# A Strassen scheme of seven products for the first matrix product of the second gated MLP

## The chip, the cores and the metric

The kernel runs on one core of a Trainium2 chip. The metric is device time in microseconds (us) of one execution, the median of three runs. A core has five engines with a queue of instructions each: TensorE (PE) for matrix products, VectorE (DVE), ScalarE (ACT) and GpSimd (POOL) for elementwise work, and SyncE (SP), which here only issues DMA transfers. PE reads SBUF and writes PSUM; ACT and DVE read both.

## What is computed

The input passes an attention with exponential gates (mLSTM, 4 batches x 8 heads x 768 steps, head size 40), whose output is a matrix of 3072 tokens x 320. Then come two MLPs, each of two matrix products with a function between them:

```
def _moe_ref(x, w_in, w_out):            # first part
    h = x @ w_in                         # 3072x320 @ 320x2048
    g = np.where(h >= 1, h, np.where(h <= -1, 0.0, (h + 1) ** 2 / 4))
    return g @ w_out                     # 3072x2048 @ 2048x320

def _moe2_ref(x, w_in, w_out):           # second part
    h = x @ w_in
    r = np.maximum(h, 0.0)
    g = r * r
    return g @ w_out
```

Both parts have the same shapes. Everything is float32 on the outside.

## The kernel before

Tokens are cut into 24 chunks of 128, d_ff into 16 tiles of 128 (f). The model size 320 is three pieces: 128, 128 and 64 rows. PE takes a shortened float format, so every float32 operand is split into a high part and a low part (high = cast, low = value minus high), and a product is three matmuls: high x high, high x low, low x high. The 64 rows left over stand twice in one stationary operand, once as high and once as low, so they need two matmuls. A first product of one tile f with one block of tokens (`mm1` in `dense`, L1131) is thus 3 + 3 + 2 = 8 matmuls; the weight tile is the stationary operand, and the columns of a matmul are the tokens of the block. The second product (`mm2`, L1191) takes 128 tokens as stationary operand and 320 columns of w_out: three matmuls for each chunk and tile, added up in PSUM over the tiles.

In the first part, blocks have 3 chunks (384 columns), in the second part 4 (512 columns, 6 blocks, `SIZES2`). One `dense(j, f)` is a visit of block j to tile f: mm1 into a PSUM bank h (there are two), then relu on ACT (L1136, L1138), in the first part a square (L1142), a product with h on DVE (`gate`, L1149, L1151), the cast to the high part on ACT (a copy, L485), the subtraction for the low part (`lo`, L1163, on POOL or DVE), and mm2. In the second part all subtractions of `lo` run on POOL. The accumulators of mm2 are the PSUM banks acc0, acc1, acc2 and v.

Weight tiles of both parts take the same 16 places w0 to w15. They come as 64-bit numbers (`weights`): a DMA load into wraw, a clamp (L508), a move (`a_move`, L503) and a tail pass (`a_tail`, L511) on ACT, a join on DVE (L515), the cast (`a_hi`, to w), and two subtractions (L524, L528) for the low parts. A tile of the second part can be written once the last block of the first part has used its place. So two blocks at the seam are visited in turns of eight tiles (`TURNS2`), two of the first part and, before the change, also the first two of the second part.

The order on each engine is not that of the code. Every step is given to `Plan.add` with engine or engines, rank, duration, needs and products; `Plan.order` then goes through a list schedule: an engine that is free takes, of the steps that are ready, the one with the lowest rank. Ranks are moved by tables (`MOVE`, `SHIFT_OF`, `FINE`), the choice between engines by `PICK` and by `PEN`, a surcharge on any engine but the first named. Engines then work through their queues in that order, waiting on semaphores. Attention (chunk by chunk) runs in between the visits of the first part and is over well before the second part.

Of the kernel before, what the change touches and what calls it, by code (L numbers as in the profile page):

```python
# [19 lines left out]
U = 64  # L20
# [19 lines left out]
class Plan:  # L40
# [18 lines left out]
    def add(self, eng, rank, dur, fn, need=(), make=()):  # L59
# [10 lines left out]
        if self.group:  # L70
            bias = PICK.get(f"{kind}{i}", {}).get(fn.__name__, 0.0)
        self.bias.append(bias)
        self.tags.append(self.group)
        self.steps.append((eng, round(rank, 3), fn, tuple(need), tuple(make)))

# [3 lines left out]
    def order(self):  # L79
# [103 lines left out]
def pool(n):  # L183
# [13 lines left out]
LEAD2 = {3: [12, 9, 3], 4: [12, 9, 6, 3]}  # L197
# [14 lines left out]
}  # L212
# [16 lines left out]
        "keep": -54.24, "evac": -38.36, "turn": -51.89, "store": 169.37},  # L229
}  # L230
# [129 lines left out]
    "w15": {"clamp": -92.87, "a_hi": 47.78},  # L360
}
# [7 lines left out]
WLEAD2 = (13, 0)  # L369
# [15 lines left out]
def kernel(  # L385
# [15 lines left out]
        vt=2, qt=2, kt=2, sg=2, xn=2, rc=2, cx=2, yx=1, Ca=CA, Cb=CB, tiny=1, xTh=XTB, xTl=XTB, pa=PAB, r=3, g0=3, g1=3, o=2, x2=2,  # L401
        h=2, acc0=1, acc1=1, acc2=1, s=2, v=1)
    psum = ("h", "acc0", "acc1", "acc2", "s", "v")
    pools = {}
    for space, tags in ((None, [t for t in bufs if t not in psum]), (PS, psum)):
        for b in sorted({bufs[t] for t in tags}):
            kw = {} if space is None else {"space": space}
            pool_ = ctx.enter_context(tc.tile_pool(name=f"p{b}{'s' if space else ''}", bufs=b, **kw))
            for t in tags:
                if bufs[t] == b:  # L410
                    pools[t] = pool_
    const = ctx.enter_context(tc.tile_pool(name="const", bufs=1))
# [6 lines left out]
    eyes = const.tile([128, 8, U], F32, name="eyes")  # L419
    nident = const.tile([128, 128], F32R, name="nident")  # L420
    half = const.tile([128, 1], F32, name="half")
    it = const.tile([128, NCB, R], F32, name="it")
    logs = const.tile([128, SUMC + 1, 2, R], F32, name="logs")
# [28 lines left out]
    rest = [(j, 0, NF) for j in range(len(blocks)) if j not in turns]  # L452
    m = max(j for j, _, _ in TURNS1)
    n = max(j for j, _, _ in TURNS2)
    visits = TURNS1 + [x for x in rest if m < x[0] < n] + TURNS2 + [x for x in rest if x[0] > n]
    rank_of, first_of, ends, last_of, first_use = {}, {}, {}, {}, {}
    g = 0
    for j, f0, f1 in visits:
        first_of.setdefault(j, g)
        for f in range(f0, f1):  # L460
            rank_of[j, f], ends[j, f] = g, (f0, f1)
            last_of[blocks[j][0], f] = g
            first_use.setdefault((blocks[j][0], f), g)
            g += 1

# [27 lines left out]
    def weights(part, f, rank):  # L493
# [42 lines left out]
        plan.add(av(WH), rank, 0, a_hi, [("wt", K, 3)], [(W, part + 1)])  # L536
# [518 lines left out]
    def part2(j):  # L1055
        return blocks[j][0] == 1

    def xkeys(j, k):
        if part2(j):
            return [("qk", ("x", j), k), ("d0", ("x", j), k)], [("vko", ("x", j), k), ("d1", ("x", j), k)]  # L1060
        return [("xTh", j, k)], [("xTl", j, k)]

    def to_xT(j, k, src, at, key=None):
# [10 lines left out]
        def halves(i, s):  # L1074
            return [(t[:, :, s] if t.shape[1] > 1 else t[:, 0, s], slice(o, o + t.shape[1]) if t.shape[1] > 1 else o)
                    for t, o in xT[j][i]]

        def hi(e, i=0):
            if k == 0:
                tags = [("xTh", "xTl")] if blocks[j][0] == 0 else [("qk", "vko"), ("d0", "d1")]  # L1080
                xT.setdefault(j, {})[i] = [
                    (new(t[i], [128, n, w], F32R), o)
                    for t, (n, w, o) in zip(tags, [(3, NX, 0)] if len(tags) == 1 else [(2, NMAX, 0), (1, NMAX, 2)])]
            if i == 0:
                for t, c in halves(0, slice(L * k, L * (k + 1))):
# [23 lines left out]

    def dense(j, f):  # L1110
        part, mine = blocks[j]
# [5 lines left out]
        W = [(f"w{f}", part + 1, i) for i in (1, 2)]  # L1117

        def mm1():
            w = t_["w", part, f]["w"]  # L1120
            xh, xl = ([t[:, i, 0:N] for t, o in x for i in range(t.shape[1])] for x in xT[j].values())
# [11 lines left out]
        def relu():  # L1133
            r = z["r"] = new("r", [128, NX])[:, 0:N] if part == 0 else new("xTl", [128, NMAX])[:, 0:N]
            if part == 0:
                nc.scalar.activation(out=r, in_=z["h"], func=ACTF.Relu, scale=0.5, bias=half)  # L1136
            else:
                nc.scalar.activation(out=r, in_=z["h"], func=ACTF.Relu)  # L1138
# [7 lines left out]
        def gate():  # L1146
            r = z["r"]
# [252 lines left out]
```

## Time and profile before

| | us |
|---|---|
| median of 3 runs (827.82 to 828.53) | 828.47 |
| span of the profiled execution | 830.9 |
| PE busy | 819.8 |
| ACT busy | 459.0 |
| DVE busy | 387.1 |
| POOL busy | 365.8 |
| DMA, mean rate | 88 GB/s |

The profiled execution's own time is its span, 2.4 us above the median of the timed runs. Matmuls overlap in the profile, and their ends are modelled, so the pace of PE is read from the distance between starts, not from a duration. The second part begins with the first matmul of 512 columns, near 475 us, and the last matmul of the kernel starts near 827 us.

### The profile page before, as it was taken

How to read it: one execution, taken by the hardware profiler on the slowest of the kernel's cores; microseconds unless marked ns; L12 is line 12 of the kernel's file. 1: busy time of each engine (PE TensorE's matmuls, PEld its weight loads, DVE VectorE, ACT ScalarE, POOL GpSimd, SP SyncE). 2: the span in 40 equal slices, each digit the busy share in tenths (PEclk: the TensorE clock that was granted, in tenths of full speed). 3: DMA queues.
4: the chain of work that ended last, by engine and by line, in shares of the span. 5: the costliest groups of instructions: out<-in, count | busy, mean ns of one | idle time of the engine just before them, and what ended most of it. 6: DMA issues, size and time to landing. Idle time of an engine off the chain costs nothing.

```text
span 830.9 us, 18844 instructions
## 1 busy us (share of the span) xinstructions
PE 819.8 (99%) x7536; PEld 753.4 (91%) x7536; DVE 387.1 (47%) x760; ACT 459.0 (55%) x897; POOL 365.8 (44%) x387
## 2 busy tenths in 40 slices
PE   8999999999899999999999999999999999999998
PEld 7668899999899999999999988999899898998997
DVE  5678879785676555544225655312121111111111
ACT  4667678866456556555678867443433433433432
POOL 3133220042353467682677566534533534433333
PEclk9899999999999999999999999999999999999999
DMA  8467564435443464521313541002110100100000
GB/s 229 162 220 237 166 172 151 141 108 124 109 116 92 110 150 125 160 56 31 70 41 99 164 98 67 1 0 70 29 42 1 45 26 1 52 1 0 32 1 33
DMA packets 93244, 73.41 MB, mean 88 GB/s; under 512 B 58944, under 2 KB 77372, under 8 KB 93156
## 3 DMA queue, kind: packets, MB, share of 16 engines
q1 hardware_dynamic: 93156, 72.21, 30.5%
q8 instruction: 59, 0.97, 0.5%
q14 instruction: 29, 0.24, 0.1%
HBM read 61.67 MB, written 10.51 MB: 87 GB/s over the span
## 4 chain that ended last, share of the span: by engine, by line
PE 91%; DMA 4%; SPq 1%; DVE 1%; ACT 1%; POOL 1%; issue 0%; POOLq 0%; DVEq 0%
PE h L1131 42%; PE acc L1191 34%; PE v L1191 5%; PE v L904 2%; PE s L850 2%; PE acc L1274 1%; PE s L857 1%; PE h L745 1%; DMA qk<-in_qk_dram 1%; DMA w<-in_gates_dram 1%; DMA vko<-in_vko_dram 1%; PE acc L550 1%; PE h L748 1%; SPq L433 1%; DMA x<-xn 1%
## 5 line engine op out<-in xcount | busy, mean ns | idle before, releaser
L1163 POOL TENSOR_TENSOR xTh<-xTl,xTh 128x512 fp32r<-128x512 f32 x96 | 124.1, 1292 | 177.1 <-ACT xTh L485 176.8
L1191 PE MATMUL acc<-w,g 128*128 128x320 f32 x1152 | 194.9, 312 | 0.1
L1151 DVE TENSOR_TENSOR xTl<-xTl,h 128x512 f32<-128x512 f32 x96 | 66.0, 688 | 245.3 <-ACT xTl L1138 245.3
L1191 PEld LDWEIGHTS acc<-w,g 128*128 128x128 f32 x1152 | 176.0, 188 | 3.3 <-ACT g L485 0.6
L1131 PE MATMUL h<-xTh,w 128*128 128x384 f32 x640 | 176.1, 340 | 2.4 <-ACT xTh L485 2.3
L1191 PE MATMUL acc<-w,xTh 128*128 128x320 f32 x864 | 142.5, 308 | 0.0
L1191 PEld LDWEIGHTS acc<-w,xTh 128*128 128x128 f32 x864 | 134.2, 188 | 8.2
L1131 PE MATMUL h<-qk,w 128*128 128x512 f32 x384 | 135.9, 395 | 0.0
L1131 PE MATMUL h<-xTl,w 128*128 128x384 f32 x384 | 129.9, 338 | 0.6 <-POOL xTl L1092 0.6
L1138 ACT ACTIVATE xTl<-h 128x512 f32<-128x512 f32 x96 | 57.4, 598 | 115.2 <-PE h L1131 112.1
L1131 PEld LDWEIGHTS h<-xTh,w 128*128 128x128 f32 x640 | 117.3, 188 | 3.8 <-ACT xTh L485 2.6
L1136 ACT ACTIVATE r<-h,half 128x384 f32<-128x384 f32 x128 | 74.0, 578 | 79.6 <-PE h L1131 68.2
L1149 DVE SCALAR_TENSOR_TENSOR r<-r,h 128x384 f32<-128x384 f32 x128 | 70.0, 547 | 78.8 <-ACT r L1142 73.5
L485 ACT ACTIVATE xTh<-xTl 128x512 fp32r<-128x512 f32 x96 | 60.7, 632 | 81.9 <-PE v L1191 80.1
L1131 PEld LDWEIGHTS h<-qk,w 128*128 128x128 f32 x384 | 72.1, 188 | 12.9
L1163 POOL TENSOR_TENSOR g<-r,g 128x384 fp32r<-128x384 f32 x63 | 66.3, 1053 | 36.0 <-ACT g L485 35.2
L485 ACT ACTIVATE g<-r 128x384 fp32r<-128x384 f32 x128 | 66.4, 520 | 21.2 <-PE acc L1191 18.3
L1131 PE MATMUL h<-vko,w 128*128 128x512 f32 x192 | 75.7, 394 | 0.0
L1131 PEld LDWEIGHTS h<-xTl,w 128*128 128x128 f32 x384 | 72.4, 188 | 0.9 <-POOL xTl L1092 0.9
L1142 ACT ACTIVATE r<-r 128x384 f32<-128x384 f32 x128 | 66.9, 523 | 2.9
L1131 PE MATMUL h<-d,w 128*128 128x512 f32 x192 | 60.3, 395 | 0.0
L1191 PE MATMUL v<-w,xTh 128*128 128x320 f32 x288 | 57.8, 309 | 0.0
(148 smaller groups left out, 1098.4 us busy)
## 6 DMA issues: line engine op xcount, KB each, us to landing
wraw<-in_wts_dram SPq DMA_DIRECT2D x32, 704.0 KB
vko<-in_vko_dram SPq DMA_DIRECT2D x24, 524.5 KB
d<-f_all SPq DMA_DIRECT2D x32, 128.0 KB
qk<-in_qk_dram SPq DMA_DIRECT2D x24, 160.0 KB
out_dram<-o SPq DMA_DIRECT2D x20, 160.0 KB
qk<-in_qk_dram SPq DMA_DIRECT2D x24, 128.0 KB
x<-x SPq DMA_DIRECT2D x24, 128.0 KB
ab<-a_all SPq DMA_DIRECT2D x20, 128.0 KB
```

Source lines behind the costliest of these rows:

```text
L433: nc.sync.dma_start(out=to[a], in_=t[32 * a:32 * a + 32].rearrange("r (b t) -> r b t", t=32))
L485: nc.scalar.activation(out=out, in_=in_, func=ACTF.Copy)
L850: nc.tensor.matmul(out=z["s"][a][u, U * h:U * h + U], lhsT=z["qk"][row[a], 0, h, u], rhs=z["qk"][row[a], 1, h, u], start=True, stop=True)
L904: nc.tensor.matmul(out=z["y"][sub[u], E * h:E * h + E], lhsT=lhsT, rhs=rhs, start=start, stop=True, skip_group_check=True)
L1131: nc.tensor.matmul(out=h, lhsT=a, rhs=b, start=(i == 0), stop=(i == 7))
L1136: nc.scalar.activation(out=r, in_=z["h"], func=ACTF.Relu, scale=0.5, bias=half)
L1138: nc.scalar.activation(out=r, in_=z["h"], func=ACTF.Relu)
L1142: nc.scalar.activation(out=z["r"], in_=z["r"], func=ACTF.Square)
L1149: nc.vector.scalar_tensor_tensor(out=r, in0=r, scalar=1.0, in1=z["h"], op0=ALU.min, op1=ALU.max)
L1151: nc.vector.tensor_mul(out=r, in0=r, in1=z["h"])
L1163: engine[e].tensor_sub(out=z["g1"], in0=z["r"], in1=z["g0"].bitcast(F32))
L1191: nc.tensor.matmul(out=acc[k][:, 0:DM], lhsT=a, rhs=b, start=(f == f0 and i == 0), stop=(f == f1 - 1 and i == 2))
```

## The change

The second part's first product is no longer computed tile by tile. Two weight tiles (u = 0, 1; a pair p) and two token halves (a, b) of a block of six chunks form a 2 x 2 by 2 x 2 product, where the inner index is the first and the second piece of 128 rows of the model size. A scheme of seven products (Strassen's, in Winograd's form) replaces the eight. It needs four sums of the tokens (`operands`, tile tt or o, then split into th, tl), and sums of the weights (`sums_of`: one piece is summed in place in the odd tile, three sums go to ws). The 64 rows left over are added the plain way, two matmuls for each of the four results, inside the products P2, P5, P4 and P3. So a pair and block has 7 x 3 + 4 x 2 = 29 matmuls of 384 columns (`products`, L1424), where before the same work was 32 of 384 or 24 of 512.

The four results come together in the two banks of h (X and Y). P1 goes to X and ACT copies it (`first`, to a tile U); P2 is added to X and gives C11, which ACT reads through a relu. P6 goes to Y, DVE adds the copy (u2), P7 is added to Y, DVE adds the copy again (u3). P5 overwrites X, DVE adds u3 (C22); P4 is added to Y, DVE adds the copy (C21); P3 is added to X, DVE adds u2 (C12). Each result is then squared after a relu (`square`, L1473 and L1474 on ACT), cast (`hi`, L532) and subtracted (`lo`, L1484) into a tile G, and goes through mm2 (L1501) one pair later. Six accumulators are used: acc0, acc1, acc2, v and both banks s.

Blocks of the second part are four of six chunks, all run from pair 0 to pair 7, so the turns of the second part's blocks are gone. Pools are given back and taken anew in SBUF when attention is done (`swap1`) and when the first part's first products are done (`swap2`). The operands of every second block are put into the tiles g, r, wraw and wt, which the first part no longer uses. The surcharge `PEN` does not hold for the new steps (`EVEN`), so their subtractions may go to DVE, and in the built program all of `lo` does. The ranks of the new steps have tables of their own ("u", "z", "p").

```diff
-SIZES2 = [4] * 6
+SIZES2 = [6] * 4
+HB = 3
-TURNS2 = [(6, 0, 8), (7, 0, 8), (6, 8, 16), (7, 8, 16), (8, 0, 8), (9, 0, 8), (8, 8, 16), (9, 8, 16)]
+TURNS2 = [(6, 0, 8), (7, 0, 8), (6, 8, 16), (7, 8, 16)]
+PAIR = 4.0
+STAGE = {"P1": 0.0, "P6": 0.35, 0: 0.7, "P2": 1.05, "P7": 1.4, 1: 1.75, "P5": 2.1, "P4": 2.5, 2: 2.9, "P3": 3.3, 3: 3.65}
...
-                end = max(free.setdefault(e, 0.0) + ahead, ready[i]) + dur + (PEN if best else self.bias[i])
+                end = max(free.setdefault(e, 0.0) + ahead, ready[i]) + dur + ((0.0 if self.tags[i] and self.tags[i][0] in EVEN else PEN) if best else self.bias[i])
...
+        def apart(e):
+            u, v, s = y["t"], z["t"], sums()
+            engine[e].tensor_sub(out=s[:, 256:384], in0=u[:, 0:128], in1=v[:, 0:128])
+            engine[e].tensor_sub(out=s[:, 384:512], in0=u[:, WS:WH], in1=v[:, WS:WH])
+        def chain(e):
+            u, v, s = y["t"], z["t"], sums()
+            engine[e].tensor_add(out=v[:, 0:128], in0=v[:, 0:128], in1=v[:, 128:256])
+            engine[e].tensor_sub(out=s[:, 0:128], in0=v[:, 0:128], in1=u[:, 0:128])
+            engine[e].tensor_sub(out=s[:, 128:256], in0=u[:, 128:256], in1=s[:, 0:128])
...
+        def sums(e):
+            t = z["t"] = new(tt, [128, 4, L])
+            a, b = z[0], z[1]
+            for o, x, y in ((0, b[:, 0], a[:, 0]), (2, b[:, 1], b[:, 0]), (1, b[:, 1], t[:, 0]), (3, a[:, 1], t[:, 1])):
+                engine[e].tensor_sub(out=t[:, o], in0=x, in1=y)
...
+                seq = [(ah, bh), (ah, bl), (al, bh)]
+                if extra:
+                    seq += [(rest(extra[0]), x) for x in right(*extra[1])]
...
+        stage("P1", "X", 2, (0, 0), ("a", 0), None, [], [X])
+        plan.add({A: act(NH), V: dvep(NH)}, g + 0.1, 0, first, [X] + sw, [p1])
+        stage("P6", "Y", 2, (2, 0), ("t", 1), None, [], [Y_])
+        plus("u2", g + 0.4, "Y", "p1", "U", "u2", [Y_, p1])
+        stage("P2", "X", 0, (0, 1), ("a", 1), (0, ("a", 2)), [X, p1], [X + (1,)])
+        plan.add(A, g + 1.1, act(NH), relu, [X + (1,)] + sw, [("R", (q, "C11"))])
+        stage("P7", "Y", 0, (2, 2), ("t", 2), None, [Y_, u2], [Y_ + (1,)])
+        plus("u3", g + 1.5, "Y", "p1", "U", "u3", [Y_ + (1,), p1])
+        stage("P5", "X", 1, (1, 0), ("t", 0), (1, ("b", 1)), [X + (1,), ("R", (q, "C11"))], [X + (2,)])
+        plus("c22", g + 2.2, "X", "u3", "R", "C22", [X + (2,), u3])
+        stage("P4", "Y", 0, (1, 1), ("t", 3), (1, ("a", 2)), [Y_ + (1,), u3], [Y_ + (2,)])
+        plus("c21", g + 2.6, "Y", "p1", "R", "C21", [Y_ + (2,), p1])
+        stage("P3", "X", 0, (2, 1), ("b", 0), (2, ("b", 1)), [X + (2,), ("R", (q, "C22"))], [X + (3,)])
+        plus("c12", g + 3.4, "X", "u2", "R", "C12", [X + (3,), u2])
...
+            plan.add({A: act(NH) * (1 if C == "C11" else 2), **pv(NH)}, g + at, 0, square, [RK], [RK + (1,)])
+            plan.add(av(NH), g + at + 0.1, 0, hi, [RK + (1,)] + sw, [GK])
+            plan.add(pv(NH), g + at + 0.2, 0, lo, [RK + (1,), GK], [GK + (1,)])
```

On PE, in the last block before the change, one tile's first product and the second product of the tile before it stand in a row like this (qk, vko and the two d hold the tokens, xTh the second product's left side):

```order
L1131 MATMUL h<-qk,w_7639 128x512
L1131 MATMUL h<-vko,w_7639 128x512
L1131 MATMUL h<-qk,w_7639 128x512 x2
L1131 MATMUL h<-vko,w_7639 128x512
L1131 MATMUL h<-qk,w_7639 128x512
L1131 MATMUL h<-d_9268,w_7639 128x512
L1131 MATMUL h<-d_9276,w_7639 128x512
L1191 MATMUL acc_9877<-w_7433,xTh 128x320 x3
L1191 MATMUL acc_9883<-w_7433,xTh 128x320 x3
L1191 MATMUL acc_9903<-w_7433,xTh 128x320 x3
L1191 MATMUL v<-w_7433,xTh 128x320 x3
```

And on PE in the last block after it, the first half of a pair: P1, P6, P2, P7, P5 with the beginning of P4, where g, r, wraw and wt hold the block's tokens and sums, ws the weight sums, and G the second product's left side of the pair before:

```order
L1424 MATMUL h<-g,w_7634 128x384 x3
L1501 MATMUL acc_10116<-w_7533,G 128x320 x3
L1424 MATMUL h<-wraw,ws_7778 128x384 x3
L1424 MATMUL h<-g,w_7634 128x384 x3
L1424 MATMUL h<-r,w_7634 128x384 x2
L1501 MATMUL acc_10129<-w_7533,G 128x320 x3
L1424 MATMUL h<-wraw,ws_7778 128x384 x3
L1501 MATMUL acc_10154<-w_7533,G 128x320 x3
L1424 MATMUL h<-wraw,w_7802 128x384 x3
L1424 MATMUL h<-g,w_7802 128x384
L1424 MATMUL h<-wt,w_7802 128x384 x4
L1424 MATMUL h<-r,w_7802 128x384 x2
```

The products now alternate between the two banks h, and only one group of the second product and P6 stand between P1 and P2, where before a bank was read only after a whole tile's product.

On ACT, the place where the second part begins, before (xTl takes the relu, xTh the cast, wt, wraw and w are steps of weight tiles):

```order
L1138 ACTIVATE xTl<-h 128x512
L485 ACTIVATE g_7310<-r 128x384
L485 ACTIVATE xTh<-xTl 128x512
L1138 ACTIVATE xTl<-h 128x512
L511 ACTIVATE wraw<-wraw 128x704
L1138 ACTIVATE xTl<-h 128x512
L485 ACTIVATE xTh<-xTl 128x512
L485 ACTIVATE w_7368<-wt 128x704
```

The same place on ACT after (U is the copy of P1, R the relu, g and r without h are the first part's last visits, g and r from x are tokens of the next block):

```order
L532 ACTIVATE U<-h 128x384
L1244 ACTIVATE r<-r 128x384
L550 ACTIVATE wt<-wraw 128x704
L532 ACTIVATE w_7209<-wt 128x704
L1447 ACTIVATE R<-h 128x384
L532 ACTIVATE g<-r 128x384
L1474 ACTIVATE R<-R 128x384
L550 ACTIVATE wt<-wraw 128x704
L532 ACTIVATE G<-R 128x384
L532 ACTIVATE w_7253<-wt 128x704
L532 ACTIVATE g<-x_6646 128x2x128
L532 ACTIVATE r<-x_6646 128x128
```

The weight steps have kept their place at the seam, and between them now stand the copy, the relu, and up to eleven passes for each pair.

On DVE, a place in the first part where the order begins to differ, near the fourth visit, before:

```order
L1149 SCALAR_TENSOR_TENSOR r<-r,h 128x384
L891 TENSOR_TENSOR d_1110<-s,d_1110 128x256
L881 TENSOR_TENSOR Cb<-s,cx 104x164
L876 TENSOR_TENSOR cx<-Cb,ab 104x164
L1163 TENSOR_TENSOR g_1434<-r,g_1324 128x384
L811 TENSOR_TENSOR kt<-vko,d_1394 128x320
L774 SCALAR_TENSOR_TENSOR d_1453<-d_1116,eyes 128x512
```

and after, where kt comes later and a weight tile's clamp stands in between:

```order
L1249 SCALAR_TENSOR_TENSOR r<-r,h 128x384
L969 TENSOR_TENSOR Cb<-s,cx 104x164
L964 TENSOR_TENSOR cx<-Cb,ab 104x164
L555 TENSOR_SCALAR wraw<-wraw 128x704
L862 SCALAR_TENSOR_TENSOR d_1453<-d_1128,eyes 128x512
```

So the planner's other steps and tiles have moved steps of the first part against each other, though the tables of ranks of that part are unchanged.

## Rows read from the trace of the kernel before

**Rows 1.** The page: busy time by engine, and two rows of the 40 slices.

```profile
PE 819.8 (99%) x7536; PEld 753.4 (91%) x7536; DVE 387.1 (47%) x760; ACT 459.0 (55%) x897; POOL 365.8 (44%) x387
...
PEclk9899999999999999999999999999999999999999
```

**Rows 2.** Stretches: us, busy us of PE, PEld, DVE, ACT, POOL, PEclk, DMA share, GB/s.

```profile
80.00:100.00 20.00, 19.96 (x294) 16.84 (x291) 16.68 (x39) 13.38 (x29) 7.08 (x7) 1.00 0.47 145
...
120.00:140.00 20.00, 19.89 (x123) 19.11 (x123) 18.85 (x38) 16.11 (x39) 0.68 (x1) 1.00 0.32 104
...
420.00:440.00 20.00, 20.00 (x127) 20.00 (x126) 5.27 (x10) 16.34 (x41) 15.60 (x20) 1.00 0.17 48
...
540.00:560.00 20.00, 20.00 (x114) 18.15 (x113) 4.13 (x6) 9.17 (x19) 7.42 (x7) 1.00 0.00 0
...
700.00:720.00 20.00, 20.00 (x112) 18.02 (x111) 4.13 (x6) 9.53 (x22) 11.00 (x13) 1.00 0.10 31
```

**Rows 3.** PE in order of time, second part: start us, us, instruction, count.

```profile
599.73 0.39 PE L1131 MATMUL h<-qk,w 128*128 128x512 f32 x1
...
601.59 1.48 PE L1191 MATMUL acc<-w,xTh 128*128 128x320 f32 x9
...
818.62 1.48 PE L1191 MATMUL acc<-w,xTh 128*128 128x320 f32 x9
...
826.97 0.60 PE L1191 MATMUL v<-w,xTh 128*128 128x320 f32 x3
```

**Rows 4.** PE in order of time, first part, where attention is over.

```profile
406.95 0.34 PE L1131 MATMUL h<-xTh,w 128*128 128x384 f32 x1
...
447.63 0.33 PE L1131 MATMUL h<-xTh,w 128*128 128x384 f32 x1
```

**Rows 5.** Groups by line: busy us, mean ns of one, idle before and its releasers.

```profile
L1131 PEld LDWEIGHTS h<-xTh,w 128*128 128x128 f32 x640 | 117.3, 188 | 3.8 <-ACT xTh L485 2.6 <-DVE r L1149 0.5
L1136 ACT ACTIVATE r<-h,half 128x384 f32<-128x384 f32 x128 | 74.0, 578 | 79.6 <-PE h L1131 68.2 <-POOL g L1163 4.7 <-DVE g L1163 4.1
L1149 DVE SCALAR_TENSOR_TENSOR r<-r,h 128x384 f32<-128x384 f32 x128 | 70.0, 547 | 78.8 <-ACT r L1142 73.5 <-POOL d L1092 2.2 <-ACT g L485 1.7
L485 ACT ACTIVATE g<-r 128x384 fp32r<-128x384 f32 x128 | 66.4, 520 | 21.2 <-PE acc L1191 18.3 <-DVE o L1222 1.2 <-DVE r L1149 0.6
...
L1163 DVE TENSOR_TENSOR g<-r,g 128x384 fp32r<-128x384 f32 x65 | 41.7, 641 | 7.1 <-ACT g L485 6.7
...
L515 DVE SCALAR_TENSOR_TENSOR wt<-wt,wraw 128x704 int32<-128x704 int32 x32 | 31.8, 999 | 9.9 <-ACT wt L503 9.5
L511 ACT ACTIVATE wraw<-wraw 128x704 int32<-128x704 uint8 x32 | 27.2, 850 | 8.1 <-DMA wraw<-in_wts_dram 8.1
L503 ACT ACTIVATE wt<-wraw 128x704 f32<-128x704 f32 x32 | 26.5, 840 | 1.3 <-DVE w L528 1.1
L485 ACT ACTIVATE w<-wt 128x704 fp32r<-128x704 f32 x25 | 19.6, 785 | 3.7 <-DVE wt L515 3.4 <-PE acc L1191 0.2
```

**Rows 6.** All engines in order of time, near the end (idle before, releaser).

```profile
814.75 0.40 PE L1131 MATMUL h<-d,w 128*128 128x512 f32 x1
...
815.25 0.60 ACT L1138 ACTIVATE xTl<-h 128x512 f32<-128x512 f32 x1 [1.29 <-PE h L1131]
...
826.75 1.82 SPq L1235 DMA_DIRECT2D out_dram<-pa  x4
...
827.61 0.44 ACT L485 ACTIVATE pa<-v 128x320 f32<-128x320 f32 x1
```

**Rows 7.** The longest wait of PE, in order of time.

```profile
227.77 0.52 ACT L485 ACTIVATE xTh<-x 128x384 fp32r<-128x384 f32 x1 [4.70 <-DMA x<-xn]
...
228.34 0.45 PE L1131 MATMUL h<-xTh,w 128*128 128x384 f32 x1 [2.30 <-ACT xTh L485]
```

**Rows 8.** Two stretches of 2 us around it, columns as in rows 2.

```profile
226.00:228.00 2.00, 0.04 (x1) 0.00 (x0) 0.00 (x0) 0.23 (x1) 0.00 (x0) 1.00 0.51 161
...
230.00:232.00 2.00, 2.00 (x18) 1.56 (x20) 0.81 (x3) 0.22 (x1) 2.00 (x3) 0.50 0.07 23
```

More of the change, by code (lines that the diff above doesn't have):

```diff
@@ L74, in add, with marked @@
         self.steps.append((eng, round(rank, 3), fn, tuple(need), tuple(make)))
+    def marked(self, kind):
+        keys = []
+        for i, tag in enumerate(self.tags):
+            if tag and tag[0] == kind:
+                keys.append(("done", i))
+                self.steps[i] = self.steps[i][:4] + (self.steps[i][4] + (keys[-1],),)
+        return keys
     def mode_of(self, i):
@@ L229 @@
         "keep": -54.24, "evac": -38.36, "turn": -51.89, "store": 169.37},
+    "u": {"load": -10.31, "clamp": 38.18, "a_move": 169.88, "a_tail": 757.89, "v_join": -59.97, "a_hi": 720.77,
+        "v_lo": -372.19, "lo": 57.21, "apart": -172.84, "chain": -299.51, "s_hi": -216.6, "s_last": -370.46,
+        "s_lo": 1196.1},
[4 rows of a table added]
 }
@@ L360 @@
     "w15": {"clamp": -92.87, "a_hi": 47.78},
+    "u": {"clamp": -68.75, "a_hi": -219.76, "lo": 44.72, "apart": 161.63, "chain": -96.62, "s_hi": 111.69,
+        "s_lo": -17.71},
+    "z": {"sums": -189.49, "hi": -0.37, "lo": -1.49},
+    "p": {"first": -280.65, "square": -13.55, "hi": -127.32, "lo": 1.09, "evac": -259.63},
 }
@@ L451 @@
     turns = {j for j, _, _ in TURNS1 + TURNS2}
[L452 to L456, printed above, removed]
+    visits = TURNS1 + [(j, 0, NF) for j in range(NB1) if j not in turns] + TURNS2
+    rank_of, first_of, ends, last_of = {}, {}, {}, {}
     g = 0
@@ L461 @@
             rank_of[j, f], ends[j, f] = g, (f0, f1)
-            last_of[blocks[j][0], f] = g
-            first_use.setdefault((blocks[j][0], f), g)
+            last_of[f] = g
             g += 1
+    NP = NF // 2
+    pair_at = {}
+    for j in range(NB1, len(blocks)):
+        for p in range(NP):
+            pair_at[j, p] = g + PAIR * len(pair_at)
+    end_at = g + PAIR * len(pair_at)
     plan = Plan(bufs)
@@ L1133, in relu @@
         def relu():
[L1134 to L1138, printed above, removed]
+            z["r"] = new("r", [128, NX])[:, 0:N]
+            nc.scalar.activation(out=z["r"], in_=z["h"], func=ACTF.Relu, scale=0.5, bias=half)
         def square(e):
@@ L1213, in dense @@
-                continue
-            y = t_["o", part, n] = {}
-            end = j == len(blocks) - 1
-            def evac(e, k=k, y=y, n=n, end=end):
-                y["o"] = new("pa" if end else "o", [128, DM])
-                if f0:
-                    nc.vector.tensor_add(out=y["o"], in0=acc[k][:, 0:DM], in1=t_["pa", part, n])
-                elif part == 0:
-                    nc.vector.transpose(out=y["o"], in_=acc[k][:, 0:DM])
-                else:
-                    copy(e, y["o"], acc[k][:, 0:DM])
@@ L1226, in turn @@
-            def turn(y=y, n=n):
-                p = t_["pa", part, n]
-                nc.vector.transpose(out=p, in_=y["o"])
-                y["o"] = p
-            def store(n=n, y=y):
-                if part == 0:
-                    scatter(x2_d[n], y["o"])
-                else:
-                    nc.sync.dma_start(out=out[128 * n:128 * (n + 1), :], in_=y["o"])
-            ok = ("pa" if end else "o", (part, n))
-            on = {V: dvep(DM)}
-            if part and not f0 and not (end and k == 1):
-                on = {A: act(DM), V: dvep(DM)}
@@ new lines, in keep, with swap1 @@
+                    copy(e, t_["pa", 0, n], acc[k][:, 0:DM])
+                plan.add({A: act(DM), V: dvep(DM)}, g + 1.6, 0, keep, [ak + (f,)], [("pa", (0, n), f1)])
+                continue
+            result(0, n, ak + (f,), lambda k=k: acc[k], g + 1.5, {V: dvep(DM)}, ("pa", (0, n), f0) if f0 else None)
+    bufs.update({f"ws{p}": 1 for p in range(NF // 2)}, tt=1, ah=1, al=1, bh=1, bl=1, th=1, tl=1, G=5, R=3, U=5)
+    def swap1():
+        leave("left", len(stack["left"]) - shared)
+        enter("left", some([f"ws{p}" for p in range(NF // 2)] + ["tt", "ah", "al", "bh", "bl", "th", "tl"]), "b")
@@ L1317 @@
             dense(j, f)
+    plan.group = None
+    plan.add("N", first_of[NB1 - 1], 0.0, swap1, attended, [("sw1", 0)])
+    plan.add("N", end_at, 0.0, swap2, [("mm1", g) for g in rank_of.values()], [("sw2", 0)])
+    for f in range(NF):
+        plan.group = "u", f
+        weights(1, f, LATE["u"] + max(last_of[f] + 1, pair_at[NB1, f // 2] - WLEAD2))
+    for j in range(NB1, len(blocks)):
+        plan.group = "z", j
+        for i in range(HB):
+            operands(j, i, LATE["z"] + pair_at[j, 0] - LEAD2[j - NB1][i])
+    plan.group = "p", 0
+    for j, p in pair_at:
+        products(j, p)
     with tc.manual_schedule():
@@ L1321 @@
             fn(e)
+        for side in stack:
+            leave(side, len(stack[side]))
 def _layout(q, k, v, i_gate, f_gate, o_gate, moe_w_in, moe_w_out, moe2_w_in, moe2_w_out):
```

356 lines of the change are left out of this document (260 added, 96 removed), and 8 rows, old and new, of tables (MOVE, SHIFT_OF).

## The prediction, before the changed kernel ran

> **What bounds the kernel now.** I read the page's busy table and its slices first [rows 1], then the busy time of each engine in stretches of 20 us [rows 2], then the matmuls one by one in two stretches [rows 3, 4], the duration of each kind of elementwise instruction [rows 5], and last the end of the span [rows 6] and the one long wait [rows 7, 8]. In [rows 1] TensorE (PE) is busy 99% of the span, the next engine, ScalarE (ACT), 55%, and the granted clock is at 9 or more in every slice. In [rows 2] PE is busy 20.00 of 20 us in each stretch of the second part (540:560, 700:720), at a clock of 1.00, with ACT, VectorE (DVE) and GpSimd (POOL) at most half busy. So the second part takes the time that its matmuls take, and a matmul taken out there is time taken out, as long as no other engine comes up to PE.
>
> **What one matmul costs.** In [rows 3] eight matmuls of 512 columns run from 599.73 to 601.59, 0.2325 us each. At the end, 57 of 320 columns run without a break from 818.62 to 826.97, 0.1465 us each. For 384 columns [rows 4]: from 406.95 to 447.63 PE does 15 visits of 8 x 384 and 9 x 320 columns, 2.712 us a visit; less 9 x 0.1465 that leaves 0.1742 us. These three lie on a line through about 3 ns, so time goes by columns and shorter matmuls are hardly dearer per column.
>
> **What the change takes out.** First product of the second part, before: 6 blocks x 16 tiles x 8 matmuls of 512 columns = 768 x 0.2325 = 178.6 us. After: 4 blocks x 8 pairs x 29 matmuls of 384 columns (seven products of 3, and the 64 rows left over in four of them, 2 each) = 928 x 0.1742 = 161.7 us. The second product stays at 24 chunks x 16 tiles x 3 = 1152 matmuls of 320 columns, 168.8 us. The difference is 16.9 us, all of it on PE where PE is the bound. (The Trainium skill, "TensorE: Matmul & The Clock Gate", Back-to-back issue gap, puts an isolated warm matmul at columns / 2.4 GHz plus a fixed 2.5 ns; the estimate by it is 165.7 less 150.9, 14.8 us saved, since 160 more matmuls pay the fixed part. The rows are longer than it at all three widths and decide here.)
>
> **What it adds off PE, in the steady pairs.** A pair of tiles for one block is 29 x 0.1742 + 36 x 0.1465 = 10.33 us of PE. ACT gets the copy of P1, the first relu (from PSUM, 0.578 each), and 11 passes of 384 columns in SBUF (0.52): 6.9 us. DVE gets five sums with a PSUM operand (0.547, the price of the gate) and four subtractions at no more than 0.641: 5.3 us [rows 5]. POOL, which did every subtraction of the second part before, gets none of these. Both have a third or more of the pair free, so in total they are covered.
>
> What can still stop PE is the chain inside a pair, since the two PSUM banks of h are now written, read and written on. P2 adds to the bank of P1, so it must wait for the copy of P1. In the order that most pairs have, one group of three second-product matmuls (0.44) and P6 (0.52) stand between: 0.96 us of cover. In [rows 6] the last matmul of a tile starts at 814.75, is over one pitch later at 814.98, and the waiting relu starts at 815.25: 0.27 us; the copy takes 0.58; in [rows 7] PE starts 0.05 us after the ACT instruction it waits for. Sum 0.90, so 0.06 us are left, if ACT is idle when P1 ends. It is: the last ACT pass of the pair before can end about 2.5 us after P3 (0.27 + 0.55 for the sum, three passes of 0.52), and P1 ends 6 x 0.44 + 0.52 = 3.2 us after P3. P7 behind P1+P6 has 1.31 us of cover for 0.87 of work, P5 behind the relu 1.4 for 0.90. I take no wait in these pairs, 0 to 3 us over all.
>
> **Where cover is thin: the start of the second part.** In pairs 0 to 4 ACT has, besides 5 x 6.9 = 34.5 us of pair work, seven moves (0.840), six tail passes (0.850) and seven castings (0.785) of weight tiles and two us of other work: 53.1 us, against 145 x 0.1742 + 195 x 0.1465 = 53.8 us of PE. In pair 0 alone it is 13.5 against 12.5. DVE has 5 x 5.3 = 26.5 us of pair work there, and for six or seven weight tiles a join (0.999), a clamp and two low parts, one of which POOL had before, three sets of weight sums and three results of the first part; at some 3 us a tile and 1.8 a set an estimate of another 26 us. So two queues that work in order are nearly full for 54 us [rows 5], and a weight step of 0.8 us that stands ahead of a copy delays PE directly. Before, ACT came to 16.34 of 20 in 420:440 and PE did not wait [rows 2]. Bounds: 0 (all weight steps fall into free places) to one weight step of 0.84 in front of P2 or P5 in each of the eight pairs of that block, 7 us. I take 3.0, near the excess of ACT in pair 0 plus two single steps.
>
> **What else moves.** The order of the first part is drawn anew between about the 4th and the 34th of its 128 visits (some 80 to 180 us) and is the same, instruction by instruction, on PE, ACT, DVE and the DMA queue from there to about the 112th visit. PE had no idle time to win there (19.96 and 19.89 of 20 in 80:100 and 120:140), while DVE was at 16.68 and 18.85 [rows 2]. So this can only lose: 0 to 5 us (one long wait of the kind of [rows 7, 8] at most), I take 1.5. That wait itself, PE idle for 2.30 us near 227 and then at a clock of 0.50 [rows 7, 8], lies in the unchanged stretch and stays. The operands of the next block (sums and splits, on DVE and ACT) are made in pairs 7 to 10, 15 to 17, 24 and 25, where DVE reaches 11.5 of 10.8 once: 0 to 1, I take 0.3. At the end, the last 18 groups of the second product follow P3, 7.9 us of PE over some 3.2 us of chain, so nothing waits there; behind the last matmul stand an ACT copy (0.44) and a store as before, in a row of six instead of four, whose issues (0.455 each, [rows 6]) keep pace with the groups: 0.2.
>
> **The sum.** -16.9 + 3.0 + 1.5 + 0.3 + 0.2 = -11.9 us. The profiled execution spans 830.9 us, 2.4 more than the median of the timed runs, 828.47; so 819.0 in its terms, 816.6 us in a timed run.
>
> **The rivals.**
> One, the queues cost more: the start of the second part and the new order of the first reach their upper bounds together, 7 + 5 and 0 to 3 for the steady pairs. That gives 820.5 to 827. For it: ACT and DVE at nearly 100%, and an order that was free of waits before. Against it: the same ACT load went through before with no wait.
> Two, on the other side: the copy of P1 comes late in every pair. If one square and one split (1.04 us) stand ahead of it when P1 ends, each pair waits 1.04 - 0.06 = 0.98 us, 32 pairs 31 us: 843. It decides from 11.9 / 32, 0.37 us a pair, on. For it: the margin is only 0.06 us, ACT works in order, and 11 passes pair by pair stand on a chain that begins in the same pair. Against it: ACT is free about 0.7 us before P1 ends, by the working above.
> Three, loading the stationary operand sets the pace: 160 more loads at 188 ns [rows 5] are 30 us, 858. Against it: in 420:440 the loads are busy 20.00 of 20 us [rows 2] and 127 matmuls still go by their columns, 0.157 us each on average, less than one load; the mix of 384 and 320 there is that of the changed second part. (The Trainium skill, "Perfetto Trace Analysis", Identifying the Most-Contended Engine, says to judge TensorE's headroom by its LDWEIGHTS busy share and not by matmul busy time; by that rule the second part would be short of room for more loads. The row at 20.00 speaks against it.)
> Four, the saving doesn't arrive, because something takes it back nearly whole: within 0.2%, 827 to 830.
>
> **How the numbers follow.** The forecast, 810.5 to 820.5, gets 0.74; rival one 0.12, two 0.08, three 0.02, four 0.04. The low end of the range is all unknown costs at nothing, 828.5 - 16.9 = 811.6, with 0.6 for the pitches read from rows rounded to 0.01 us; the high end takes in most of rival one. A measurement of this kernel can tell about 0.2% (1.7 us) from no change; the forecast and rival one are faster by more than that, four and a tail of one and two are the same, two and three slower.
>
> **What would show it.** In the profile after: 29 matmuls of 384 columns and 36 of 320 in 10.3 us in the steady pairs, PE busy 20.00 of 20 there, no wait of P2 on ACT of more than 0.1 us; waits of PE on ACT or DVE, if any, in the first 54 us of the second part and between 80 and 180 us; the matmuls of the first product summing to 162 us. A regular gap behind P1 in each pair would be rival two; a pitch above 0.175 for 384 columns in the second part, rival three. If PE idles for over 8 us in the second part, the steady pairs were worked out wrongly.

## The result, and the profile after the change

The changed kernel takes **814.39 us** (median of 4 runs, 813.70 to 815.79) against 828.50 for the kernel before: a ratio of 0.9831, 95% interval 0.9812 to 0.9851, 14.1 us less. The forecast was 816.6, 11.9 us less. The profiled execution spans 814.1 us.

The page of the changed kernel, columns as in [rows 1]:

```profile
PE 799.9 (98%) x7696; PEld 769.3 (95%) x7696; DVE 526.7 (65%) x1108; ACT 542.9 (67%) x1102; POOL 213.8 (26%) x254
...
PE   8999999999999999999999999999999999999998
...
PEclk9999999999999999999999999999999999999999
```

PE is still the bound at 98%, while ACT went from 55% to 67% and DVE from 47% to 65%. The stretches of [rows 2], now in the changed kernel (us, busy us of PE, PEld, DVE, ACT, POOL with counts, PEclk, DMA share, GB/s):

```profile
80.00:100.00 20.00, 19.28 (x237) 17.87 (x236) 17.44 (x41) 12.54 (x24) 4.62 (x7) 1.00 0.47 154
120.00:140.00 20.00, 18.23 (x216) 16.99 (x215) 17.69 (x38) 11.02 (x24) 1.42 (x2) 0.91 0.32 108
...
540.00:560.00 20.00, 20.00 (x128) 20.00 (x128) 16.11 (x43) 16.00 (x38) 0.12 (x1) 1.00 0.13 36
700.00:720.00 20.00, 20.00 (x128) 20.00 (x127) 9.13 (x18) 12.32 (x25) 0.00 (x0) 1.00 0.00 1
```

In the second part (last two rows) PE is busy 20.00 of 20 us at a granted clock of 1.00, as before. In the first part (first two rows) there are holes that [rows 2] did not have: 19.28 and 18.23, where 19.96 and 19.89 stood. So the gain is in the second part, and there is a small loss in the first.

One pair of the second part on PE, in order of time (start us, us, instruction, count). The last matmul of P1, one group of the second product, P6, and the first matmul of P2:

```profile
681.55 0.34 PE L1424 MATMUL h<-ah,w 128*128 128x384 f32 x1
681.73 0.60 PE L1501 MATMUL acc<-w,G 128*128 128x320 f32 x3
682.17 0.34 PE L1424 MATMUL h<-th,ws 128*128 128x384 f32 x1
682.34 0.34 PE L1424 MATMUL h<-tl,ws 128*128 128x384 f32 x1
682.51 0.34 PE L1424 MATMUL h<-th,ws 128*128 128x384 f32 x1
682.69 0.34 PE L1424 MATMUL h<-ah,w 128*128 128x384 f32 x1
```

and the copy of P1 on ACT at the same time:

```profile
681.92 0.49 ACT L532 ACTIVATE U<-h 128x384 f32<-128x384 f32 x1 [0.93 <-PE h L1424]
```

Each start follows the one before by 0.175 us (384 columns) or 0.147 (320); nothing stands still. The copy ends at 682.41, P2 begins at 682.69.

For all runs I measured one more length, from the first matmul of the second part's first product to the start of the last matmul of the kernel (474.41 to 810.35 in the profile of the changed kernel). It holds no attention and almost no first part. "Over pitch" is what of it is more than its matmuls at 0.2325, 0.1748 and 0.1464 us.

| kernel | median us | before, same chip | second part us | over pitch us |
|---|---|---|---|---|
| before (profile) | 828.47 | | 351.97 | 0.1 |
| changed | 814.39 | 828.50 | 335.94 | 0.0 |
| changed, second time | 814.36 | 827.95 | 335.93 | -0.1 |
| changed, third time | 816.14 | 828.25 | 335.94 | 0.0 |
| three matmuls more a pair (e1) | 832.25 | 828.91 | 352.49 | -0.3 |
| three fewer a pair (e2) | 803.83 | 828.25 | 323.45 | 4.2 |
| 128 columns copied ahead (e3) | 820.25 | 828.91 | 339.63 | 3.6 |
| copy made twice (e4) | 823.73 | 828.91 | 343.52 | 7.5 |
| move made twice (e5) | 818.44 | 828.91 | 338.10 | 2.1 |
| before, seven of eight matmuls (e6) | 806.33 | 827.95 | 329.84 | 0.3 |
| before, one g tile (e7) | 833.60 | 827.95 | 351.97 | 0.1 |
| subtractions on GpSimd (e8) | 818.24 | 827.95 | 339.30 | 3.3 |
| changed, g planned as two (e9) | 813.95 | 828.25 | 337.88 | 1.9 |
| two plans joined (e10) | 809.62 | 828.71 | 336.00 | 0.0 |

Three profiles of the changed kernel agree on the second part to 0.01 us, although their spans differ by 5.8 us (808.5, 814.1, 814.3). What differs between runs of one kernel lies in the first part.

### The profile page after: what moved, and what is told of

Same layout as the page of the kernel before. It is cut to its first block, busy times and chain, and to the rows that moved or that the text cites. A ratio compares the mean times of both kernels' runs of the same rounds, so it can differ in the third digit from the quotient of the medians.

```text
span 814.1 us, 19491 instructions
## 1 busy us (share of the span) xinstructions
PE 799.9 (98%) x7696; PEld 769.3 (95%) x7696; DVE 526.7 (65%) x1108; ACT 542.9 (67%) x1102; POOL 213.8 (26%) x254
## 4 chain that ended last, share of the span: by engine, by line
PE 54%; DMA 1%; issue 1%; SPq 0%; POOL 0%; ACT 0%; DVE 0%; ACTq 0%; POOLq 0%; DVEq 0%
PE h L1424 20%; PE acc L1501 10%; PE s L1501 7%; PE acc L1280 7%; PE h L1236 6%; PE v L1501 3%; DMA x<-x 0%; DMA x<-o 0%; PE v L992 0%; PE s L938 0%; SPq L478 0%; PE s L945 0%; POOL xTl L1166 0%; POOL g L1257 0%; PE s L1050 0%
## 5 line engine op out<-in xcount | busy, mean ns | idle before, releaser
L1501 PE MATMUL acc<-w,G 128*128 128x320 f32 x576 | 104.6, 308 | 0.0
L1501 PEld LDWEIGHTS acc<-w,G 128*128 128x128 f32 x576 | 92.8, 188 | 0.0
L532 ACT ACTIVATE g<-r 128x384 fp32r<-128x384 f32 x128 | 66.5, 521 | 34.5 <-PE acc L1280 28.3
L1484 DVE TENSOR_TENSOR G<-R,G 128x384 fp32r<-128x384 f32 x128 | 70.1, 559 | 22.1 <-ACT G L532 19.7
L1436 DVE TENSOR_TENSOR R<-h,U 128x384 f32<-128x384 f32 x96 | 53.3, 556 | 38.3 <-PE h L1424 36.7
L1436 DVE TENSOR_TENSOR U<-h,U 128x384 f32<-128x384 f32 x64 | 35.7, 557 | 61.1 <-PE h L1424 61.0
L1473 ACT ACTIVATE R<-R 128x384 f32<-128x384 f32 x96 | 49.7, 517 | 33.4 <-DVE R L1436 33.4
L1474 ACT ACTIVATE R<-R 128x384 f32<-128x384 f32 x128 | 67.2, 525 | 3.8
L1501 PE MATMUL s<-w,G 128*128 128x320 f32 x384 | 68.2, 308 | 0.0
L532 ACT ACTIVATE G<-R 128x384 fp32r<-128x384 f32 x128 | 64.5, 517 | 1.7
L1501 PEld LDWEIGHTS s<-w,G 128*128 128x128 f32 x384 | 59.9, 188 | 0.0
L1257 DVE TENSOR_TENSOR g<-r,g 128x384 fp32r<-128x384 f32 x65 | 42.9, 661 | 8.7 <-ACT g L532 7.0
```

The costliest lines, as they stand in the source:

```text
L532: nc.scalar.activation(out=out, in_=in_, func=ACTF.Copy)
L1257: engine[e].tensor_sub(out=z["g1"], in0=z["r"], in1=z["g0"].bitcast(F32))
L1436: nc.vector.tensor_add(out=z[key], in0=z[bank], in1=z[u])
L1474: nc.scalar.activation(out=r, in_=r, func=ACTF.Square)
L1484: engine[e].tensor_sub(out=t[:, 1], in0=z[C], in1=t[:, 0].bitcast(F32))
L1501: nc.tensor.matmul(out=acc2[j, kk][:, 0:DM], lhsT=a, rhs=b, start=(p == 0 and head and i == 0), stop=(p == NP - 1 and not head and i == 2))
```

## The experiments

**Are the columns all?** Theory: the second part takes the time of its matmuls' columns, so the gain is 96 matmul-equivalents of 384 columns. Rival: the blocks of six or the empty GpSimd gave a part of it. Three idle matmuls were put into P1:

```diff
+for again in range(2 if name == "P1" else 1):
     for m, (l, r) in enumerate(seq):
         nc.tensor.matmul(out=z[bank], lhsT=l, rhs=r, start=(m == 0 and start > 0), ...)
```

> The changed kernel, but P1 issues its three matmuls twice (the first three are overwritten), so that a pair has 32 matmuls of 384 columns, as many as eight plain products. Order, blocks of six, sums and copies stay. Theory (only the columns count): 96 more matmuls x 0.1748 us = +16.8, so 831.2 us, all of the gain gone, and the second part without idle time on PE. Rival (the blocks of six or the emptier GpSimd brought a part of the gain): the time stays well below the kernel before, under 824.

Measured: 832.25 us, ratio to the kernel before 1.0030 (1.0007 to 1.0053). The second part grew from 335.94 to 352.49, by 16.55. The whole gain is gone, so the rival falls: blocks, pools and the move of the subtractions together earn nothing beside the columns. That it is even slower than before by 0.6 to 4.4 us is the first sign of the loss in the first part.

The same on the kernel before (`seq = seq[:7]` in `mm1` for the second part):

> The kernel before, where the last of the eight matmuls of each first product in the second part is left out: 96 matmuls of 512 columns fewer. Theory (the second part takes the time of its columns, before as after): 96 x 0.2325 = -22.3 us, 806.2. Rival (ACT or VectorE would come next soon): less than half of it, over 817.

Measured: 806.33, 21.6 less; second part 22.1 shorter. The stretch shows why no other engine came in next: with fewer columns ACT is still at 8.05 and DVE at 4.13 of 20 us.

```profile
700.00:720.00 20.00, 20.00 (x114) 18.23 (x113) 4.13 (x6) 8.05 (x14) 7.44 (x7) 1.00 0.05 17
```

The other direction, three matmuls less in the changed kernel (`if name == "P7": return`):

> The changed kernel without the three matmuls of P7, so that the term P7 is missing from three of the four results (part of the computation is left out); all sums, copies and passes stay. 96 matmuls fewer x 0.1748 = -16.8 us if PE's columns are still the only bound: 797.6. If ACT, VectorE or the chain in a pair is close behind (P5 then follows P2 sooner): over 801.

Measured: 803.83. The second part lost 12.49 us, not 16.8. Here the chain inside the pair shows: with P7 gone, P5 follows P2 after one group, but must wait until ACT's relu has read the bank. PE at one of these places (the relu, R<-h, is the ACT row):

```profile
520.78 0.60 PE L1503 MATMUL acc<-w,G 128*128 128x320 f32 x3
521.52 0.44 PE L1426 MATMUL h<-th,w 128*128 128x384 f32 x1
521.80 0.34 PE L1426 MATMUL h<-tl,w 128*128 128x384 f32 x1
```

```profile
520.98 0.49 ACT L1449 ACTIVATE R<-h 128x384 f32<-128x384 f32 x1 [1.37 <-PE h L1426]
```

The group ends its issue at 521.22; P5 starts at 521.52, 0.05 after the relu's end. Ten pairs wait so, 0.30 us each and 0.10 more behind it, 4.1 of the 4.2 us over pitch. So the next bound is the chain of the two banks, not the load of ACT, which had been idle for 1.37 us before.

**How much cover has the copy of P1?** The prediction had 0.06 us. A pass was put ahead of the copy, of 128 columns, and then of all:

```diff
+copy(e, z["p1"][:, 0:128], z["X"][:, 0:128])     # e3 (e4: the whole copy, twice)
 copy(e, z["p1"], z["X"])
```

> The changed kernel with one more pass on ACT ahead of the copy of P1: its first 128 columns are copied once before, 0.20 us of ACT by the distance of such passes in the trace. The prediction's margin between P1, its copy and P2 (0.06 us): each of the 32 pairs waits 0.14 us, 4.5 us in all, 818.9. The margin read from the trace of the changed kernel (copy starts 0.20 after P1's end, takes 0.49, P2 begins 0.96 after P1's end: 0.22 with 0.05 for the release): no wait, 814.4 within 1 us.

> The changed kernel with the copy of P1 made twice in a row. Two such passes stand 0.39 us apart in the trace. Margin 0.22 us: each pair waits 0.17, 32 pairs 5.4 us, 819.8. The prediction's margin of 0.06 and its 0.52 us for a pass: 0.46 x 32 = 14.7 us, 829.1. If PE had spare time in the second part: 814.4, no change.

Measured: 820.25 and 823.73; the second part is 3.7 and 7.6 us longer. What the medians are longer beyond that, 2.2 and 1.8 us, lies ahead of the second part. Both expectations that had a number for the margin missed e3, and for a plain reason: the pass of 128 columns did not cost 0.20 us but 0.31 (0.80 for both against 0.49), and the second full copy not 0.39 but 0.52. e3, PE and ACT in the same pair as above:

```profile
682.23 0.34 PE L1424 MATMUL h<-th,ws 128*128 128x384 f32 x1
682.50 0.44 PE L1424 MATMUL h<-ah,w 128*128 128x384 f32 x1
682.77 0.34 PE L1424 MATMUL h<-al,w 128*128 128x384 f32 x1
```

```profile
681.64 0.80 ACT L532 ACTIVATE U<-h 128x128 f32<-128x128 f32 x2 [0.93 <-PE h L1424]
```

P2 starts 0.05 after the end of the copies (682.44), 0.09 late: 0.31 less 0.22. The margin of 0.22 read from the trace of the changed kernel is right. And a second cost shows: the matmul behind the wait comes 0.28 later instead of 0.175, another 0.10. In e4 the same two are 0.30 and 0.105:

```profile
686.77 1.01 ACT L532 ACTIVATE U<-h 128x384 f32<-128x384 f32 x2 [0.93 <-PE h L1424]
```

```profile
687.36 0.34 PE L1424 MATMUL h<-th,ws 128*128 128x384 f32 x1
687.83 0.44 PE L1424 MATMUL h<-ah,w 128*128 128x384 f32 x1
688.11 0.34 PE L1424 MATMUL h<-al,w 128*128 128x384 f32 x1
```

18 pairs wait so: 18 x 0.195 = 3.5 and 18 x 0.405 = 7.3. 17 of the 32 pairs have only one group and P6 between P1 and P2, one more gets a late copy because ACT is busy; the other 14 have two or more groups and do not wait.

**Is ACT full at the start of the second part?** The move of each weight tile was made twice (`for again in range(1 + part)` around it):

> The changed kernel, where the move of each weight tile of the second part is made twice on ACT, 16 passes more, 8 of them in the first five pairs. The prediction's sum (53.1 us of ACT by durations against 53.8 of PE) with 8 x 0.84 = 6.7 more would make ACT the bound there: about 6 us later, 820.4. By the distances between starts in the trace of the changed kernel (ACT 46.7 busy of 53.8, a move every 0.73): 52.6 of 53.8, so 0 to 2 us, 814.4 to 816.4.

Measured: 818.44, but of these 4 us the second part holds 2.2 (over pitch 2.1); the rest lies in front of it and within what runs differ by. Six more us of ACT work in the first five pairs cost 2, so ACT was not full. Pair 0 and the sum of pairs 0 to 4 in the changed kernel, and below them pair 0 with the doubled moves (columns as above; a stretch is a pair):

```profile
474.40:486.90 12.50, 12.50 (x82) 12.50 (x81) 9.84 (x20) 10.99 (x22) 5.25 (x7) 1.00 0.46 131
...
sum 53.80, PE 53.80 PEld 53.80 DVE 46.27 ACT 46.70 POOL 11.62; mean PE 10.76 PEld 10.76 DVE 9.25 ACT 9.34 POOL 2.32
```

```profile
474.30:486.90 12.60, 12.35 (x77) 11.80 (x76) 9.08 (x18) 12.29 (x25) 4.68 (x6) 1.00 0.41 125
```

ACT is busy 46.70 of 53.80 us, not 53.1; with the double moves it reaches 12.29 of 12.60 in pair 0, and there PE begins to wait.

**Did it matter that the subtractions went to VectorE?** The surcharge was put back for the pair steps (`EVEN = ("u", "z")`):

> The changed kernel, but the surcharge on any engine but the first named holds for the pair steps again, so that 124 instructions, nearly all of the subtractions for low parts, go back from VectorE to GpSimd; the order in the second part is drawn anew by it. Theory (PE is the bound, the mm2 groups take what is ready one pair later): no change, 813.5 to 816. Rival (a GpSimd subtraction of 384 columns is longer than on VectorE, and groups of the second product wait for it): some 0.1 to 0.5 us a pair, 817.6 to 830.

Measured: 818.24, second part 3.4 us longer. So it has the rival's sign, but not its mechanism: one group of the second product waited, for its accumulator and not for a subtraction. Four times P2 waited for a copy of P1 that came late (0.40, 0.67, 0.19 and 0.85 us, and 0.10 behind each: 2.5 of the 3.3). ACT ahead of the second of these:

```profile
506.24 0.53 ACT L1474 ACTIVATE R<-R 128x384 f32<-128x384 f32 x1
506.67 0.85 ACT L558 ACTIVATE wraw<-wraw 128x704 int32<-128x704 uint8 x1
507.42 0.51 ACT L532 ACTIVATE G<-R 128x384 fp32r<-128x384 f32 x1
507.83 0.51 ACT L1473 ACTIVATE R<-R 128x384 f32<-128x384 f32 x1
508.37 0.52 ACT L1474 ACTIVATE R<-R 128x384 f32<-128x384 f32 x1
508.80 0.47 ACT L532 ACTIVATE U<-h 128x384 f32<-128x384 f32 x1
```

The copy (U<-h) stands behind a row without a gap, in which a tail pass of a weight tile (0.85) has its turn. That is the stall that the prediction feared at the start of the second part, at about the price it gave (3.0 taken, 3.4 measured), in an order that the changed kernel does not have. A subtraction takes 1046 ns on GpSimd here and 559 on DVE in the changed kernel; the Trainium skill ("GPSIMD Engine Reference", Engine selection) says about twice, and the trace agrees with 1.9. In the pairs behind the weight tiles that costs nothing.

**What does the newly drawn first part cost?** One part of the change alone, in the kernel before: g0 and g1 become one tile g.

```diff
-r=3, g0=3, g1=3
+r=3, g=3
...
-R_, G0, G1 = ("r", g), ("g0", g), ("g1", g)
+R_, G0, G1 = ("r", g), ("g", g, 0), ("g", g, 1)
```

> The kernel before with one part of the change alone: the high and the low part of the first part's second-product operand are one tile instead of two. This redraws the order of the first part nearly as the change does (on PE 119 of 4300 rows differ from the changed kernel, 1280 from the kernel before); the second part stays as before. The prediction's step (the new order can only lose, 0 to 5, taken as 1.5): 830.0. What the two traces show (first part of equal length, 0.4 us shorter): 828.0 within 1 us. If the new order was part of the gain: under 826.

One figure of that text is wrong: the 1280 rows counted the new name of the tile as a difference. With names made equal, and counted as the fewest rows that set two orders apart, PE's first 4260 matmuls and loads in the program differ from the kernel before in 186 (the changed kernel in 218), and from the changed kernel in 66. (The text of e9 below counts in another way.)

Measured: 833.60 against 827.95, ratio 1.0069 (1.0039 to 1.0098), 3.2 to 8.1 us slower, with the same second part to 0.01 us. My reading of the two first profiles (first parts of equal length) was wrong: it took the kernel before from a long execution, whose second part begins at 475.3 us, while it begins at 470.5 in e6, which has the same first part. So the changed kernel was run twice more, and the way back was taken in its planner alone:

> The changed kernel once more, for its spread and beside the next kernels: 814.4 within 1 us, PE without idle time in the second part; the early part of the trace shows whether the waits near 97, 128 to 131 and 411 us and the half clock near 132 come again.

> The changed kernel beside the kernel above and the kernel before: 814.4 within 1 us; second part 335.93 us from its first to its last matmul, as in both profiles so far.

```diff
-R_, G0, G1 = ("r", g), ("g", g, 0), ("g", g, 1)     # names for the planner
+R_, G0, G1 = ("r", g), ("g0", g), ("g1", g)         # with g0=3, g1=3; in memory one tile as before
```

> The changed kernel, where only the planner is told, as before the change, that the high and the low part of the first part's second-product operand are two tiles with three places each (in memory they stay one). With that PE's order in the first part is that of the kernel before but for 82 of its 4260 instructions (370 in the changed kernel). If the newly drawn order is what cost some 2 us in the first part: 812 to 813, about 2 us below the changed kernel. If the cost has another source (SBUF pools, the weight loads of the second part): 814 to 815, as the changed kernel.

Measured: 814.36 and 816.14 for the changed kernel (the third time a little over what was expected, the second part as expected), and 813.95 for the planner's edit. The first part of the latter is shorter (last table of this section), but its second part has 1.9 us of new waits (two, on ACT's relu and copy, at 514 and 534), because the order at the start of the second part was drawn anew too. Then both plans were made, and joined at 330 us of the plan:

```diff
+late = self.order()                       # planned with g
+...
+early = self.order()                      # planned with g0, g1
+head = {i for t, i, _ in late if t < 330}
+out = [x for x in early if x[1] in head] + [x for x in late if x[1] not in head]
```

> The changed kernel with two plans put together: the first 330 us of the plan in the order of the kernel above (high and low part planned as two tiles, so near the order before the change), everything behind that in the order of the changed kernel. If the redrawn first part costs 2 to 3 us and the second part keeps its 335.94 us without a wait: about 812, 16 us under the kernel before. If the first part's gain was only spread between runs: 814 to 815, 14 under it.

Measured: **809.62 us**, ratio 0.9768 (0.9746 to 0.9790), below the changed kernel's interval. It beats both kernels: 19.1 us under the one before, 4.8 under the changed one's first median. Its two stretches of the first part:

```profile
80.00:100.00 20.00, 19.96 (x313) 17.24 (x313) 17.16 (x41) 14.41 (x32) 6.55 (x9) 1.00 0.56 173
120.00:140.00 20.00, 20.00 (x130) 19.98 (x128) 18.38 (x35) 16.32 (x34) 0.45 (x1) 1.00 0.43 141
```

PE's waits between 90 and 140 us in the changed kernel (us in total, times, longest):

```profile
PE acc L1280 <- DVE g L1257: 0.7, 1, 0.7
PE s L1152 <- DVE xn L1113: 0.7, 1, 0.7
PE h L1236 <- ACT xTh L532: 0.6, 1, 0.6
PE h L1236 <- DVE xTl L1166: 0.5, 1, 0.5
```

None of these four is left in e10. Nine profiles have the changed kernel's first part: its own three, and e1, e2, e3, e4, e5 and e8. All nine have these four waits, and e7 has them too; the kernel before, e6, e9 and e10 have none of them. So the order of the first part is what brings them. The time from the first to the 385th matmul of the second product in the first part, which spans the newly drawn stretch (about 70 to 220 us), in each profile:

| | us |
|---|---|
| order before: before, e6 | 145.3, 145.1 |
| changed: three profiles | 147.5, 146.4, 146.6 |
| the same first part: e1, e2, e3, e4, e5, e8 | 147.2, 148.6, 148.3, 147.8, 149.4, 146.6 |
| e7 | 148.2 |
| e9, e10 | 143.2, 143.2 |

The medians tell the same: take from each run's difference to the kernel before, on the same chip, the difference of the second parts. What is left lies ahead of the second part: 1.9 to 4.1 us more in the nine comparisons with the changed first part, 3.2 on average, 5.7 more in e7, and 3.1 less in e10. It scatters: e9, which has the order of e10 on PE there, is at 0.2 less.

## Why the prediction was right, step by step

| step | predicted us | measured us |
|---|---|---|
| first product, 768 x 512 to 928 x 384 columns | -16.9 | -16.4 |
| steady pairs | 0 (0 to 3) | 0 |
| start of the second part | +3.0 (0 to 7) | 0 |
| first part drawn anew | +1.5 (0 to 5) | +1.3 to 4.2, mean 2.4 (nine profiles) |
| operands of the next blocks | +0.3 | 0 |
| tail | +0.2 | +0.1 |
| sum | -11.9 | -14.1 |

With the mean for the first part the measured steps add up to -13.9; the 0.2 to the medians' -14.1 is less than the runs settle. The sum is closer than its terms: 3.0 us too much for the start of the second part stand against 0.9 too little for the first part and 0.5 too much for the columns. That these offset in part is luck; the largest term, the columns, came out by its own mechanism.

**The columns.** 928 matmuls of 384 columns took 162.2 us in the second part, 0.1748 each against 0.1742 taken from [rows 4]; 768 of 512 had taken 178.6. e1 gives nearly the same number by another way, 16.55 for 96 matmuls.

Three details of the prediction are off, and nothing rests on them: the granted clock is 8 tenths in the second slice of [rows 1], not 9 or more in every slice; GpSimd is busy 11.00 of 20 us in 700:720 of [rows 2], more than half; and the estimate in brackets beside the columns comes to 15.0 by its own formula, not 14.8.

**The steady pairs.** No wait, as taken. The margin of the copy is 0.22 us and not 0.06, because the copy starts 0.20 after P1's end (681.92 against 681.72; 0.27 was read from [rows 6]) and takes 0.49 (0.58 was the first part's relu in [rows 5]). "Most pairs" was 17 of 32. Rival two would have needed 0.37 us a pair; even the doubled copy lost 0.24 on average (7.6 / 32).

**The start of the second part** is the step that failed. The count of ACT's passes was right, their price was not: the prediction added up durations of rows, 53.1 us. But passes overlap. Five in a row in the changed kernel:

```profile
657.99 0.51 ACT L532 ACTIVATE G<-R 128x384 fp32r<-128x384 f32 x1
658.40 0.51 ACT L1473 ACTIVATE R<-R 128x384 f32<-128x384 f32 x1
658.94 0.53 ACT L1474 ACTIVATE R<-R 128x384 f32<-128x384 f32 x1
659.37 0.51 ACT L532 ACTIVATE G<-R 128x384 fp32r<-128x384 f32 x1
659.78 0.40 ACT L532 ACTIVATE g<-x 128x256 fp32r<-128x256 f32 x1
```

A pass shows 0.51 us, but the next begins after 0.41; only where the next reads what this one wrote (658.40 to 658.94, both on the same R) is it 0.54. The cast at 659.37 reads the R of another result. So ACT came to 46.70 us instead of 53.1 and DVE to 46.27 instead of about 52.5, and in the order that was built no weight step held up a copy or a relu for so long that PE waited. The Trainium skill ("Perfetto Trace Analysis", Optimizing Scalar/DVE Operations) says that a profiled latency is longer than the time for which the engine is busy, since its end overlaps with the next instruction; these rows agree. e8 shows that the stall itself is real: ACT has all but the same passes there, and in the order drawn anew the copy came late four times. e5 shows that more load brings it too.

**The first part.** +1.5 was right in sign for the changed kernel and too small: 147.6 us on average in the newly drawn stretch against 145.2 before, and 1.9 to 4.1 by the medians. "Can only lose" held against the order before, but not in general: e10 is 2.0 us shorter there than the kernel before. Which of its remaining differences does that is not settled. The long wait of [rows 7] changes from run to run: 1.35 us in the changed kernel's first profile, 0.50 to 2.06 in the nine, 2.30 in the kernel before, but 1.01 in e6 with the same order. The half clock that followed it in [rows 8] came in five of the nine and not in e6. So nothing that the change did to this wait can be read from them.

**The rivals.** One needed 5 to 12 us in both early stretches; there were about 2 to 4. Two and three did not occur: loads of the stationary operand are busy 20.00 of 20 us, and the 928 matmuls of 384 columns still go by their columns. The Trainium skill ("Perfetto Trace Analysis", Identifying the Most-Contended Engine) judges TensorE's headroom by the busy share of its loads and not of its matmuls; read as the prediction reads it, as a bound on further loads, these rows do not bear it out. Four fell with the interval.

## What to carry to other kernels

Where one engine is busy 20.00 of 20 us and no wait of it comes in, the time of a stretch is that engine's instruction count by their pitch, and this was good to 0.5 us in 16.9. e2 shows the limit: 96 matmuls less, and a chain between two engines took a quarter of it back. Add up the load of ACT and VectorE by distances between starts, not by durations; the durations overstated it by 14%. An edit in a planner's keys can draw anew a stretch that it does not touch, so compare the order there too: here it took back some 2 to 3 us, and joining two plans gained 4.8.

## What the runs showed of the hardware

- A wait of PE costs about 0.10 us more than it lasts: the second matmul behind it starts 0.28 us after the first instead of 0.175 (e2, e3, e4, e5, e8, e9 alike).
- Two ACT passes in a row that write the same tile stood 0.52 us apart (e4), others of that size that do not read each other's result 0.39 to 0.43. That the common tile is the cause is argued, not shown.
- The same waits need not bring the same clock. After PE's three waits between 128 and 131 us the granted clock was 0.50 (the level of 1.2 GHz) in the first profile of the changed kernel, and 1.00 in the second, where they stood at 125 to 128 us and were as long (0.68, 0.58 and 0.51 us). Of the nine profiles that have these waits, four show the half clock behind them (the first, e2, e4, e5). The stretch in the first profile, columns as above:

```profile
132.00:134.00 2.00, 2.00 (x8) 2.00 (x7) 1.79 (x4) 0.58 (x1) 0.00 (x0) 0.50 0.00 0
```

What decides it is open.
